# Fourier mixing and a squared-ReLU MLP on one core: a fourth x buffer, other load slots, the first x piece by SyncE's queue, and a new table

## The chip, the cores and the metric

The kernel runs on one core of a Trainium2 chip. The core has TensorE for matmuls (PE, with the weight load PEld shown apart), VectorE (DVE), ScalarE (ACT), GpSimd (POOL) and SyncE (SP), and 16 DMA engines that all DMA queues share. DMAs are issued here from two places: SP's queue (q1 in the profile, "hardware_dynamic") and POOL's queue (q0, "software_dynamic"). Only POOL's DMAs change the type on the way. The metric is device time of one execution in microseconds; lower is better.

## The reference

For each of 8 batches of 3008 rows by 256 columns: a real FFT along the rows, a complex 256 x 256 product with a bias, a soft threshold at 0.01 on the real and the imaginary part, and the inverse FFT. All 24064 rows then pass an MLP with 2048 hidden columns whose activation is `s * relu(h)**2 + b`.

```python
X = np.fft.rfft(x, axis=1)
Yr = Xr @ w_r - Xi @ w_i + b_r
Yi = Xr @ w_i + Xi @ w_r + b_i
Y = np.sign(Y) * np.maximum(np.abs(Y) - 0.01, 0)      # Yr and Yi alike
y = np.fft.irfft(Y, n=3008, axis=1)
r = np.maximum(y @ w_in, 0.0)
out = (s * (r * r) + b) @ w_out
```

## The kernel before

The FFT of 3008 points is split as 94 x 32. Each batch's x is held as 94 partitions (index n1) by 32 x 256 elements in fp16, in four chunks of 8 of the 32 positions. The first step is a matmul with A_t (94 x 96, the 94-point transform); the second goes through a detour in DRAM (u is written, read back as rows in `us`), is transformed with F_t, mixed with the weights, thresholded, transformed back with T_t, and goes through DRAM again (v written, `vs` read) to the last transform with C_t, which leaves yt, the MLP's input.

The program has two parts. `first_batch` does the whole transform of batch 0 while nothing else can run. It opens with 40 matmuls on a tile of ones (`keep_awake`), then eight groups of matmuls, one for each half chunk of x of batch 0, in that order, by edges that tie each group to the one before (`issue_after`), with five matmuls on ones behind each. ACT and DVE copy the result (ut) out. After the fourth group `place_w` copies w_st to W_t on ACT and the second part of F_c is loaded; after the sixth the big tables T_t, F_t and F_2 are loaded by SP, and F_t's landing gates POOL's loads of batch 1's x and of the MLP weights. Then comes the mix of batch 0 and what follows it.

`emit_load_x(0)` issues batch 0's x from POOL, eight pieces of 94 rows by 1024 columns, fp32 in DRAM and fp16 in the tile. Just ahead of it, A_t is issued on SP. Chunks 0 to 2 come from a pool of three buffers (`xpool`), chunk 3 from one of its own (`x2pool`). The pool `rpool`, tag "rt", has three buffers of 4 KB a partition: the two staging tiles w_st, then b_st, then the three `rt` tiles of the MLP's relus.

The second part is a loop over 47 tiles of the MLP (up to 512 rows each), 16 slots a tile, 752 slots in all, about 1.02 us each. Matmuls of the MLP are interleaved with those of the next batches' transforms: `plan` holds units of work by slot, `aside` holds loads by slot. `mark[b]` is the slot at which batch b's MLP tiles begin. In the loop that fills them, s0, s1 and s2 are the marks of batches b-2, b-1 and b; `s1_units(b)` are the first-step matmuls, `take_rows` the loads of `us` rows, `s23_units` the middle steps and `s4_units` the last. `load_x_later(b, c)` issues a chunk as two half-chunk DMAs from POOL.

What is not a matmul in this part (bank copies, relus, squares, the sums of a seven-product scheme for the second MLP matmul, stores, loads) is handed to `later` as a piece. The long string TURNS gives each piece, two characters in base 36, the engine that does it (ACT, DVE, SP or POOL) and how many pieces later it is emitted. From there each engine's order is as written (`manual_schedule`). The tag `psh` holds the first MLP matmul's two banks, `rt` the relu, `gt` its square; `s` and `gt` sums are DVE's or, as an accumulating DMA, POOL's (line 1317).

Of the kernel before, what the change touches and what calls it, by code (L numbers as in the profile page):

```python
# [11 lines left out]
F32 = mybir.dt.float32  # L12
# [14 lines left out]
    "1x1x261s291p1t221o291s1w291l1u2m2q2y321c1t1c1c25191c291d1s1c282w1o1t1k20353n6z3r6f173r111521"  # L27
    "101c0x111515141h1l14181k3o181l1x5m5m750x151h1l2e2q1u1i0g0t0g0s7x0p0t11192y1q2226080w2g0h110l"
    "111h1p3e2m2u220h0t0g1c0x1h212d2i2q3a3q0h101g0g250h3q4q0l191l1x2m3m321q0c0w1g0c0p0x1d292x3q32"
    "3y36101w091e0c0p1h0o390x1h1p252m323q3a0k0s1831523i0l0x111l1t212e2u3m36080m0c0w0k1829182o1519"  # L30
    "1h1t362u3m260o0s1p101s111h1l1x263a2i2q15321k2g154e3q0o151d25292t45453l0c0k1k0l0t1h21292h292l"
    "2t081e0d0i0g3h0h0s212h143i1g1m1k1n371g1s2g1h3e4m101a2i2q3m3q0w120s0x1s113q101p0x111g1l1m181h"
    "1g1k201l3i4y1h1m252t1c3x1h191c451c1c20191e1x11143p1x191k2814151c1q192q141o2g1d1l1k2h1h4u1c1p"
    "1p1o1x2d2p1g1x4236181824152e1865141l11161e1x2h143415182p1b1c301t151i181p291d141p1h1k291p1o24"
    "1l1n6j1k2d1l1l1k1o1h2p1x261h1t1c1w1f5v1h1p1x2d2m2u2y3i101g0x160w1h2h0x2l0w181d0x1n1o2o1t110s"
    "1t1z1x1l1x292d2u2i3e2y0g1w1110182d182p1d1g1w1d1f5b1p1o202p1l1x1g1x1h2y1g1o1h292t454i564i5a18"
    "1u0o180l0u0h1l29101g0l143h0r111g2s1d0p0s1f1p0w142l111h184a191l21252d2u2m3u2u0w200w3q0w1h100t"
    "101t1c201p2p113t141i1p26191g1w1d1t1w281x261f4b1d1h252l1h25393h4q423i4214240l0k6y0r0s3u0s2k0t"
    "0l0o0z0l0t0w1l1011141o2k191h1p293p4l294l292t1x2p0g0u0k200l0w1i0l102d0x1t0x19264i1e102y1g2h0w"
    "1g1y1k28192q1i15292t181k2k1h151e3e3m1f2k2u142s1h0x1l1d141p18191g1t2m2a1o1y1o2g1d1p1s291p1p24"  # L40
    "1p2y1o1t1s1y1o211p1q252h1k1o2w1t1k1z1k1s3g1t1l1o1z1x1h1s291p1p1q1o1x241k1t242o1p3e1l1p1o1p2h"
    "1p2t1c1l2y1h1g2h1d1i1g1w1h1m252l1o2g1l2t391j1g311t1d1620291n1d141o1h1w1w1x20241p3f7b1l1t1l1x"
    "1o1s1d1p2h461h1p1c1s1b5v191l1t213q262e2u0w1g0t0y0w1h2h0x2t0w181d0x1n1s1w1p0x0w1t1n1p1p1t2l2p"
    "3a3m2m3q0w1g150w191g14291t181s191b5j1x1h1k1w1x211h1p252a1k1o1h252l495m4i4q4y0x1q0w180t0y111l"
    "2d101g0x0w190z15142g1h0x141j1h101l3c142h1k46191h1p252l3u2u3u2u0o0w111a0w28190x181918202d3l11"
    "191d3a253a191g1k1d1l1o201l1q174b19251x2d1d2t3d3l3u4m3y460o1g0x0o4i0z0k3u182w0p0h0k0v110p0o18"
    "0w1519181w191h292h3h2x4d4d4l49292h0l3a0o1w0d0o120l0o210p3x0k111a1y1e0t6m0s2c0w102a1c1x1d3a2a"
    "1a1m0x1x2p181c2s1l1c1m363u1j282m0s2k190p2t150w1l190x14282m4i191i1428111l1l211t2l1c1t2q1g2l1h"
    "1q1c1s191i2h2t1d1k3d1p1g1v1g202s1x1h181z1p1g1o2k1l1x1q1s1t211o1w202s1x1m1t1x1o1w2p1l1x1l1t2y"
    "1t1k281l1q1o211l1q252l1o381l2c351j1g2x1x191a1c1x1r1h18251l1s1w1w24281p1r7b1x251h1p1o2o1p1x1l"  # L50
    "3u1g1t1g2k1f5v1d1h1l1t22262y2i0s1d0t2y0o1p2h0w2t0w281d0p1j0w2k1p0x101t1n1p1p2d2h3l3u424a4m08"
    "1s0t0x0w1h101p1p141k11137719181c1w191d1c1l1p3m1o2k1d1l1p293q463a260w160w1g0x260t1t2h182g0p0t"
    "290z1514251x11181z251k1s2o1g211s3m1d1p1t252d3e3m42260w18112e1g2s100t1c151g1t113d193p1c1q1x36"
    "191c1p1h1k1k241l1u1b4r181l212d1l2l353p4e4u4i3q0s380t0s160z0k160s1c150t0s171d11101t101d1k1o24"
    "1l1p1x2t41413d3d2t4h393h0w160w1c0l0t0y0p142l11450l11524m3q1m1y0u005y042410101e101p151u1i120t"
    "1t2h1014281h181i3a3e2p2d2m0o2h190l3l150w140x11141k2m3u1t1y1c28191d1g211d3d1w1h2q1g1l1k1q1g1t"
    "1h22292t1c1g3c1x1g231g1k341x1d1k231p1g1k2k1l1p1q1p1t2h1o1t1s2s1p1q1s1x1o1s251p2h1l253y1k1k28"
    "1h2a1k1x1h1i212h1k3c1h242l1f1c2w1x15161g211r1p18241p1t2g1s1t2c1x1n7f1g1x1x1h1s2o1p1p1x4e1g1t"
    "1c2k1f5z1d1h1l1t2u1y2e3e0s1d0t1i0o1p2h0w2x0w341d0p1j0w1o1t0x101d1r1p1p1x2d2d2q362m3e0c1w0t10"
    "102g181d211g211d1f5b211o1o3h1p291k1t1h1q1c1s1l1p2t454i5e4q4y151a0s1g0t160s1p29101g0p103t0r11"  # L60
    "1g2o1d0p0s1f1h0w1g2c0w19192a1d1h252l2x4m3m322q111c103e18240x111415141s1t2h0x3h151q1t2e15141s"
    "1g1p202g1p1y1f4j1h1p252p1l292x3t4i4q423m142c0l0k0y0r0w3y0w240x0p0s0z190x0w280x191c1c2o1d1l1p"
    "25412x2d4d2p3t3t250o2u0o210l0x3u0l0o350p210k1d2q0s0y0o2p0w141m182c1d221g292p1c1o2w1l1o1y3a3a"
    "452d2m1429190p2h150w1s0x1114281u3y1t221828191h1o1x1l21201p2y1c241l1u1g1x1d1u2h2t1k1s3o1p1d1v"
    "1g1o2k1x1h1k1z1x1l1c2l1p1t1m1t1w241l1s212k1p421o1t1k1o2g2h351d1h1q1c1d211c261g1s1d1i212d1o34"
    "1p202l351c301p155y181t1j19101p1h1k211p1o241x1n771g251l1l1k1s1h1p214q1h1t1c1s1b5v1d1h21253q32"
    "2i260s140p0u0l212h0w1l0s180p0t2t1c2g1p0x1c1l1n1p1h252l393u3e3y46081g0x0w191g141t19182d19135b"
    "1d141c1w191t1c1x212y1g291h1p2h3x4q564a3q0s1u0s180p0u0s1h1x101k0x142x0v0x1g2k1h110s311d141828"
    "191l1l6e1l1p1x2h2t3a4e3m2q0w19103i101k180t0s11181s1d2h0x3x141e1h2y0x181o151l1s201h1q174b1925"
    "252h192x3d3p3y4u4e3y0o340d0w4a0n0o0y0o180t0l0o0z1d0t0s1p10191g1k1w1h1x2d2p49354h414h412p2d0d"  # L70
    "120o180l0s2a0p101o0x410h1p565a1u080u0h2c0o0s1q181x19222a362u121a0p1p2d0w102w1d141e363e252c2m"
    "0k28110h2x110o281w11151h2q2y1x261g28151l1c251h2d1l1x2y1k1o212a1k1x1h26252t181g301t1k1z1k1k2w"
    "1x1h1k2x1p1g1p2k1k1l1m1p1o2g1l1t1s2s1p3u1l1p1p1o2g1l1p1g253a1h1h211c2e1g1s1d1i21291o2g192l2p"
    "1j1k2o1l1d5m20291f151c201h1p251o1o201l1o2p1x1l1k1s1l3h1l3e1h1p1c1o1h1l1t2132363e2a0w1k0t0y0w"
    "1p21182p1c2k1t15231c3g211h181t391p1t1x252h323q322e0s0w1110151g10291t1g25151l201k1x2l311o1x1p"
    "3a1c1o1h2h454h525i5a4e111q0o180p0y0k1h1p141k0p141d0v19183119111f1h0w141c1o1x1519252935424a3i"
    "320o1o103y101g11151d1c1k0x1h112h1p2y19102c181c1x191y1c25252h1l2t393h4q4a3i3q0s2k111b0o4m0o10"
    "110p140z111d0w201d141c2c191h1p2h353d3l392h293l290g1o0l0p0u0l0o2c0t2h1d461i1u220o28151x261g1t"
    "1d2i221q212l20142g1518223a3e2d1c2h1l0t1n1d1g1w1h1g1p363a1k1s1l1p1s211h1l1l1u1k1t1w211t222h2t"
    "1k1o3c1p1h1v1g1o3d251h1k231h1g1k291l1p1p1o2g1o1s212o1l1k211p1o2o1p2l1k1p1u1l1p291k4d411k1w1h"  # L80
    "1m1x291k24191j1g2h1p191x1l1c1w1d1g251o281p1x1o1x21251x261g241o211p1y252h1o2c1l1r1o2o1x1h391t"
    "1k1o1p1p1t1s1w1p1t1w2d1l1t1x221k211s1w1x2225291s2t1d1r1s2g1t1l1v1l1o211t1w241s2g1p1t1s281p1p"
    "212a1l1x1o1w1x2225251s2c1d2h1o2g1p1h1v1l1s241t1t1x1w201t1x20291p1t1t2e2y1u1u321c1l1o1s1l1q21"
    "291o2g191n1s2o1t1l2t1p1o1o1p1p1t1s2c1p1t1s251p1t212u1o1t1s1w1p1u25291o2t1d1r1s2s1t1l1v1l1o1s"
    "1t1t241s2h1p1t1t1s1t1y1w281s251p1q1x1y21261p1u1x1y"
# [64 lines left out]
def kernel(  # L150
# [51 lines left out]
    xpool = ctx.enter_context(tc.tile_pool(name="xp", bufs=3))  # L202
# [154 lines left out]
    def emit_load_x(b, chunks=range(N2 // XCH)):  # L357
        xv = x[b].rearrange("(n1 n2) d -> n1 (n2 d)", n2=N2)
        for c in chunks:
            if b < 2 and c == N2 // XCH - 1:  # L360
                t = x2pool.tile([P, XCH * D], F16, name="x2", tag="x2")
            else:
                t = xpool.tile([P, XCH * D], F16, name="x16", tag="x16")
            parts = 2 if b == 0 else 1
            w = XCH * D // parts
            for i in range(parts):
                nc.gpsimd.dma_start(
                    out=t[0:N1, i * w : (i + 1) * w],
                    in_=xv[:, c * XCH * D + i * w : c * XCH * D + (i + 1) * w],
                )  # L370
            x16[(b, c)] = t
# [12 lines left out]
    A_t = cpool.tile([P, 96], F16, name="A_t")  # L384
    nc.sync.dma_start(out=A_t[0:N1, :], in_=A_d)
    emit_load_x(0)
# [375 lines left out]
    def s1_units(b, more_banks=False):  # L762
# [6 lines left out]
        def unit(i):  # L769
# [6 lines left out]
            assert b < 2 or (b, c) in held[-3:]  # L776
# [729 lines left out]
    for c, at in enumerate((18, 18, 18, 55)):  # L1506
        aside.setdefault(at, []).append(
            lambda c=c: load_x_later(2, c, [] if c else [row_loads[(1, 3)]])
        )
# [4 lines left out]
    for b in range(2, B):  # L1514
# [4 lines left out]
        for q, at in enumerate((-9, -6, -1, 4)):  # L1519
# [6 lines left out]
        if b + 1 < B:  # L1526
            free_at = 37 + 4 * (mark[b] - s1 - 50) // 16
# [59 lines left out]
```

## Time and profile before

| | us |
|---|---|
| median of 3 runs (814.24 to 814.68) | 814.51 |
| the profiled execution | 814.47 |
| its span, first to last instruction | 812.4 |

| engine | busy us | share of the span |
|---|---|---|
| PE (matmuls) | 801.9 | 99% |
| DVE | 760.4 | 94% |
| ACT | 748.9 | 92% |
| POOL | 108.7 | 13% |

The profile is of one execution. A matmul's busy time overlaps with its neighbours', since matmuls are pipelined, so PE's 99% is a share of time in which some matmul is under way. A line such as "L225 PE MATMUL psf<-x,A_t" names the code line, the engine, and the tiles written and read; nearly all matmuls carry line 225, the helper's, and are told apart by their tiles. A wait "PEld L225 <- DVE gt L1325: 3.9, 9, 0.6" reads: weight loads waited for DVE's operation of line 1325 on gt, 3.9 us in total, 9 times, 0.6 us the longest. In a timeline an operation has its start, its length, its engine and, in brackets, how long its engine stood before it and for what. A line of a stretch gives its length, each engine's busy time with its number of instructions (PE, PEld, DVE, ACT, POOL), the granted clock of TensorE as a share, the busy share of the 16 DMA engines (over 1 where packets overlap) and GB/s.

### The profile page before, as it was taken

Reading aid. Unit: us, or ns where it says so; the run is one execution under the profiler, and the core shown is the slowest. Engines: PE = TensorE matmul, PEld = TensorE weight load, DVE = VectorE, ACT = ScalarE, POOL = GpSimd, SP = SyncE. Lnnn points to the kernel's source line nnn. Section 1 sums busy time; section 2 is a strip of 40 time slices with the busy share of each in tenths; the row PEclk is TensorE's granted clock in tenths of the full one; section 3 lists DMA queues with packets and bytes.
Section 4 is the critical chain, followed back from the end, with each engine's and each line's share of the span. In section 5 each row is a group of like instructions: output and inputs, shape, how many; then the busy total and the mean of one; then the engine's idle time right before and its main releaser. Section 6 shows DMA issues by size and latency. Waiting matters only on the chain.

```text
span 812.4 us, 22159 instructions
## 1 busy us (share of the span) xinstructions
PE 801.9 (99%) x9006; PEld 614.0 (76%) x9006; DVE 760.4 (94%) x1334; ACT 748.9 (92%) x938; POOL 108.7 (13%) x153
## 2 busy tenths in 40 slices
PE   8999999999999999999999999999999999999998
PEld 7857767777777967788677886778867788777876
DVE  5899999999999999999998999999999999999895
ACT  5989989999999999999999999999999999898884
POOL 4540000111111110121001210001100100010100
PEclk9999999999999999999999999999999999999999
DMA  8964385566856669467575875657654544632323
GB/s 201 182 173 89 92 243 150 115 138 166 222 122 120 151 154 232 100 123 179 121 209 113 158 153 145 169 125 143 140 162 117 141 98 115 176 70 54 78 55 90
DMA packets 121054, 113.42 MB, mean 140 GB/s; under 512 B 9965, under 2 KB 98161, under 8 KB 120953
## 3 DMA queue, kind: packets, MB, share of 16 engines
q1 hardware_dynamic: 102409, 80.55, 35.9%
q0 software_dynamic: 18544, 31.47, 24.0%
q8 instruction: 70, 1.15, 0.6%
q14 instruction: 31, 0.25, 0.1%
HBM read 53.52 MB, written 46.66 MB: 123 GB/s over the span
## 4 chain that ended last, share of the span: by engine, by line
PE 55%; DVE 3%; DMA 1%; issue 0%; DVEq 0%
PE psh L225 24%; PE psa L225 20%; PE psf L225 11%; DMA gt<-gt 1%; DVE gt L1325 1%; DVE ost L1390 1%; DVE ring L924 1%; DVE gt L1165 0%; DMA out_dram<-ost 0%; DVE v L288 0%; DVE u L288 0%; DVE s L1325 0%; DVE rt L1156 0%; DVE ost L1278 0%; DVE ring L907 0%
## 5 line engine op out<-in xcount | busy, mean ns | idle before, releaser
L225 PE MATMUL psh<-yt,w_in 128*128 128x512 f16 (+3 forms) x1792 | 444.5, 343 | 0.2 <-ACT rt L1154 0.2
L225 PEld LDWEIGHTS <-gt 128*128 128x128 f16 x4400 | 306.5, 98 | 143.8 <-DVE gt L1325 3.9
L1154 ACT ACTIVATE rt<-psh 128x1024 f32<-128x1024 f32 x347 | 355.0, 1025 | 25.6 <-PE psh L225 22.9
L1163 ACT ACTIVATE gt<-rt 128x1024 f16<-128x1024 f32 x259 | 272.2, 1061 | 3.4 <-DVE rt L1156 1.4
L225 PE MATMUL psa<-w_out_t,gt 128*128 128x128 f16 (+1 forms) x2208 | 199.9, 224 | 0.3 <-DVE gt L1165 0.3
L225 PEld LDWEIGHTS <-w_in 128*128 128x128 f16 x1824 | 151.9, 98 | 15.9 <-issue 1.5
L225 PE MATMUL psa<-T_s,gt 128*128 128x128 f16 x1824 | 144.2, 219 | 0.3
L1165 DVE TENSOR_TENSOR gt<-rt 128x1024 f16<-128x1024 f32 x117 | 141.2, 1217 | 2.5 <-ACT rt L1154 2.1
L1317 POOL DMA_DIRECT2D gt<-gt x65 | 56.5, 868 | 574.2 <-DVE s L1325 157.7
L1390 DVE SCALAR_TENSOR_TENSOR ost<-psa,s_bc,bias_bc 128x256 f32<-128x256 f32 x152 | 72.8, 479 | 7.8 <-PE psa L225 6.7
L1325 DVE TENSOR_TENSOR gt<-gt 128x1024 f16<-128x1024 f16 x107 | 73.0, 683 | 0.6
L1390 DVE SCALAR_TENSOR_TENSOR ost<-psa,s_bc,ost 128x256 f32<-128x256 f32 x129 | 61.7, 478 | 4.8 <-PE psa L225 4.0
L880 DVE TENSOR_TENSOR ring<-psf,s 128x512 f16<-128x512 f32 x84 | 57.6, 686 | 4.0 <-PE psf L225 2.5
L1325 DVE TENSOR_TENSOR gt<-gt,s 128x1024 f16<-128x1024 f16 x86 | 59.0, 686 | 1.2 <-PE psf L225 0.4
L1325 DVE TENSOR_TENSOR s<-gt 128x1024 f16<-128x1024 f16 x86 | 58.8, 683 | 0.4 <-ACT gt L1163 0.2
L225 PEld LDWEIGHTS <-s 128*128 128x128 f16 x688 | 45.4, 98 | 17.6
L225 PE MATMUL psa<-T_s,s 128*128 128x128 f16 x688 | 52.4, 219 | 0.0
L225 PE MATMUL psf<-W_g,xf 128*128 128x256 f16 x336 | 50.4, 273 | 0.0
L225 PEld LDWEIGHTS <-xf 128*128 128x128 f16 x504 | 44.8, 98 | 3.3
L350 POOL DMA_DIRECT2D x<-in_x_dram x48 | 32.3, 766 | 78.6 <-PE psa L225 39.6
L225 PE MATMUL psf<-x,A_t 94*96 94x512 f16 x103 | 39.3, 381 | 0.3 <-DVE u L288 0.2
L225 PE MATMUL psf<-C_t,vs 96*128 96x96 f16 x484 | 38.3, 205 | 0.9 <-DMA vs<-vd 0.6
(116 smaller groups left out, 839.4 us busy)
## 6 DMA issues: line engine op xcount, KB each, us to landing
out_dram<-ost SPq DMA_DIRECT2D x74, 256.0 KB
gt<-gt POOLq DMA_DIRECT2D x65, 256.0 KB, 4.0
ud<-u SPq DMA_DIRECT2D x56, 192.0 KB
us<-ud SPq DMA_DIRECT2D x28, 384.0 KB
vd<-v SPq DMA_DIRECT2D x42, 256.0 KB
vs<-vd SPq DMA_DIRECT2D x28, 384.0 KB
x<-in_x_dram POOLq DMA_DIRECT2D x56, 188.0 KB, 5.6
ring<-ring SPq DMA_DIRECT2D x120, 64.0 KB
```

What stands on the lines that cost most here:

```text
L225: return nc.tensor.matmul(out, lhs, rhs, **how)
L350: nc.gpsimd.dma_start(out=t[0:N1, i * w : (i + 1) * w], in_=xv[:, at : at + w])
L880: lambda e: nc.vector.tensor_tensor(out=ring[0][:, i % 4], in0=ps, in1=hold[i // 2][:, i % 2].unsqueeze(1).to_broadcast([P, 2, D]), op=ALU ...
L924: lambda e, o=o[:, k], a=a[:, k]: nc.vector.tensor_copy(out=o, in_=a),
L1154: nc.scalar.activation(out=rt, in_=ps, func=AF.Relu)
L1163: nc.scalar.activation(out=gt, in_=rr, func=AF.Square)
L1165: nc.vector.tensor_tensor(out=gt, in0=rr, in1=rr, op=ALU.mult)
L1317: nc.gpsimd.dma_start(out=a12, in_=a11, accum_op=ALU.add)
L1325: nc.vector.tensor_tensor(out=out, in0=a, in1=b, op=op)
L1390: ins = nc.vector.scalar_tensor_tensor(out=out(), in0=hold[of], scalar=s_bc[0:size], in1=other(), op0=ALU.mult, op1=ALU.add,)
```

## The change

There are four parts.

- `xpool` has four buffers in place of three, and the check that a chunk is still held looks back four chunks.
- The very first piece (batch 0, chunk 0, first half: 94 rows by 1024 columns) is loaded as fp32 by SP's queue into a staging tile x_st from `rpool`, and then converted to fp16 on chip: ACT copies the left half of its columns, DVE the right half. `emit_load_x(0)` now stands ahead of A_t's load, so x_st is the first DMA on SP's queue and A_t the second. POOL issues the other seven pieces as before.
- The loads are put at other slots: the last chunk of batch 2's x at slot 24 in place of 55; the third and fourth `us` row loads at -4 and -1 from the batch's start s1 in place of -1 and +4; the next batch's x chunks at -8, -6, 10 and 26 in place of 10, 14, 26 and some 48.
- TURNS is another table of the same length, 2693 pieces.

```diff
-    "1x1x261s291p1t221o291s1w291l1u2m2q2y321c1t1c1c25191c291d1s1c282w1o1t1k20353n6z3r6f173r111521"
...
+    "1t1t221o251l1p1y1k251o1s251h1q2i2q362q181p18181t151820181p1c203o1l201g1l294f7b1b3b1b3j15151h"
...
-    xpool = ctx.enter_context(tc.tile_pool(name="xp", bufs=3))
+    xpool = ctx.enter_context(tc.tile_pool(name="xp", bufs=4))
...
             for i in range(parts):
+                if (b, c, i) == (0, 0, 0):
+
+                    x_st = rpool.tile([P, w], F32, name="x_st", tag="rt")
+                    nc.sync.dma_start(out=x_st[0:N1], in_=xv[:, 0:w])
+                    for copy, q in ((nc.scalar.copy, 0), (nc.vector.tensor_copy, 1)):
+                        r = slice(q * w // 2, (q + 1) * w // 2)
+                        copy(out=t[0:N1, r], in_=x_st[0:N1, r])
+                    continue
                 nc.gpsimd.dma_start(
...
     A_t = cpool.tile([P, 96], F16, name="A_t")
+    emit_load_x(0)
     nc.sync.dma_start(out=A_t[0:N1, :], in_=A_d)
-    emit_load_x(0)
...
-            assert b < 2 or (b, c) in held[-3:]
+            assert b < 2 or (b, c) in held[-4:]
...
-    for c, at in enumerate((18, 18, 18, 55)):
+    for c, at in enumerate((18, 18, 18, 24)):
...
-        for q, at in enumerate((-9, -6, -1, 4)):
+        for q, at in enumerate((-9, -6, -4, -1)):
...
-            free_at = 37 + 4 * (mark[b] - s1 - 50) // 16
-            for c, at in enumerate((10, 14, 26, free_at)):
+            for c, at in enumerate((-8, -6, 10, 26)):
```

More of the change, by code (lines that the diff above doesn't have):

```diff
@@ L26 @@
 TURNS = (
-    "1x1x261s291p1t221o291s1w291l1u2m2q2y321c1t1c1c25191c291d1s1c282w1o1t1k20353n6z3r6f173r111521"
[L28 to L85, printed above, removed]
+    "1t1t221o251l1p1y1k251o1s251h1q2i2q362q181p18181t151820181p1c203o1l201g1l294f7b1b3b1b3j15151h"
+    "101p1x0w11150w201h0w14182w192h3h5m564v7j590l0p0x111m12221i000h042c7h0d0l0p0t1u121a1y040o1o08"
@@ new lines @@
+    "0p0d0t19213e262e2q050p0w2c0l1519212a2y3a2e080s280c0l2t3y4a090p0t1h2a2y2i1m081029090l0t1h2529"
+    "3m4e2q2e0w1g002i040o191c3811191h1x3i2u1y420o0w181p4y260h0t0x1d1h1x262u361y04360s180p0x2p141s"
+    "11151d1h3e2q2a2u0g111l0w1g111h1t292e3e2e2q0t360s182p363e0l0x19191h413p2x31080w1t0c0p151t2d2d"
+    "352t35081e080q0c350k0w1k2k101y111a1c1k1l2k2d2i32141e2i2u3i4i0w160t0s1p153i101o0x1x141g1i151g"
+    "1l1k1s1h3m4y191i1t2p111s1t10181v15203s141m1x0x102l1p191p2t14181c1m1d2q101c341f63191l1c1s1h3e"
@@ new lines @@
+    "175n1d1d1h181l212l3u0x1h1q2y0s0s1w0p260s450s1d0t0y161l210w2w0x1w2h0z0w2k1h0t0w1h3t1d0w1w1d1l"
+    "1s1l1p201t1j5z1c1l1l1l1k1o1h1x1l321g1p1g2c1h1h1p212i36222i0s1s0p0u0s2d2l1g310p340x1517141s1x"
+    "19101h1v1t1x252935423m4a320g1p0x0w101c101p15141k150z5r1l15181w1d21181l192y1k2k1h1h1p2d3e2i3q"
+    "2q0s3q0o110p0y0k1l2d0w1k0t0w3t0z151s2d1p0x0w1v1l1c1s201g1x1l3q191l1t1x2h3m3a4m2e0s180w161828"
+    "0x11141518201529151p196q1t1y19181s1c1h1s241h1q1h21212h19212l3d463y4m3a10240d0c4a0n0o0y0o2d11"
@@ new lines @@
+    "0l0o13150p0s1k0w0x101k2k191h1p2149354d3125312d250c2y0g100h0p0y0p102g1t3d0h1p4i2a1u0c0u0g2k0w"
+    "1d2i1g25151e1m11212h0w1g2c1d1g1q3a3u3l2d2m0s2g190l1d11101l101114282e3y191i1420111h1l1x1l2p1g"
+    "1p1y1c1g1h1u1k24191u2d2h1d1o3k1d1h1j1k1o2k1t1h1g1r1h1p1g2k1h1l1m1p1x2h1j5v1c1l1k201h3y1f5z1c"
+    "1p1d1c1o1t251615192q1d141w151a181l15161t29182w191c291b182w1l1114211j1h101t1d1o291p1o241l1n6z"
+    "1k1t1l1t1k1t1l2h1t1y1c1l181o1h1x25293m2q2y260w1g0t0y0w1x29102h14240p0x39102g1p0x101h1n1p1h1p"
@@ new lines @@
+    "29313q363q3y0c1k0x0w1019181x15141g150z6z1l19181o1p1x151l213a1g1k1d1l1x1x2a363e3m0w3q0w180l1y"
+    "0s1l2d14380h0l150r11142s1l0x141r1h141h2s1c251d421h1h1p2d2h3y3i2u2e0o0x0w3m101s0x0l0w1h0w1k21"
+    "2d0l3t0x2m1l260t0w1k141h1s241d1q1h1l2h2x1h1x293h463m464e10240h0g460r0s120s30190x0o17190t0w1l"
+    "101114182k191h1p212x4d2h2x3p1t1t2d0g6e0k1s0h0s2i0h0s2g1l3p0l111u164e0o420s290p191i141w111a1i"
+    "1m1u0p1p290k142o1d141i3a3a3h2d2i0k2c150d1d110k1t1d0x0w202q3u1x26142011191c25191l1w1h2y1c1s1g"
@@ new lines @@
+    "1q1p24151q2d2p181d381l1c1r1c1w2x1t19181v1l1c1l2g1g1p1i1o1o2h2j6f1d1h1g2o1d1e1f631g1l1c1g2k1d"
+    "1p2215191i1h14211d1i1k1s191i1t1x1g3015292917182x19111o21130t0w1p191o2c1o21281h1j771c2d1h1l1o"
+    "2k1d1h1t1y181l182c1h1l252d2m3m2m2u0w1k0t0y0p1p2h0t2l0w281d0p1n0w2k1t0x0w1p1r1p1p1x2l35424a3i"
+    "320c1l0t1010180x311h101c110v5b191g0w1h112d181p1x22101g19293p414e4m5e4u0w1m0w180l0u0l191l142w"
+    "0l0k0x0r0x0w30190p0w1f1p0s0w290x1d1g6q151d1t2d3h4u3y423e0w150w4u0w1c0s0t0w11141c0t1x0t290p2u"
@@ new lines @@
+    "113u0h0g100k11181k151q111x1x2l0x212x3d4i423e3q0g20050s460f0s3q0s2w0x0l0k0z150t0s1h0w0x10141s"
+    "191h1x254l2x3l292p3d3p2p0h1q0o100l0o0y0p142c39410l0x221m4m0y1y4m081y08250h112i101w0x1a1i1m0s"
+    "1t2d0s1c281d1c1m3q3u3125560s20150d1b11141h1l1118202a3y101a101w111d1h1o1h1t1h1p2q181l1c1m1c1o"
+    "1h222d2p1d1g351l1d1r1c1k2w1t1d1g1z1l1c1g2s1k1p1i1p1o1w1n6b1h1l1x2k1h3i1f4z1c1h181c2819292m11"
+    "151e140x201016181p191m1p251c301d2d2x1f101c1d0t1s2131150w1s191p281k1k241h1j771d1p1t1l1o2g1l1t"
@@ new lines @@
+    "1h321c1l1c2g1d1h1p2d2u323i2a0s190p0u0s1p2h0w2h0w1w1d0p1j0w381t0x1g1p1r1t1l1x2d353q3y4a320c0s"
+    "0t10111d143d1h101c110v571910182g1519181l192q14281d1h4d4l4u5i525i0t120o110l1210191t142s0l0k0x"
+    "0r0t0s2o150t0s170x0o0w2h0x1h142i0t191d252p3q463q4q0o1k0w4q0s1g150t111h141c2d2l0t290x1215260l"
+    "0o140t1g1k1w1h221h1x252l1925313h3q4a3y4e142c0l0k1m0r0s120s34110p0w171h11101p1419181g201h1p1x"
+    "252x3l3t2x311x3h1t0p4q0o100l0o3q0p0w2c1t3h0l0p320k0y0k250w191i181w0x1a11212p101k2w1l1k1y3a3u"
@@ new lines @@
+    "1j2c2m102g190l1d150w211g1115282e2i1c1m1824151h1l291p2p1k1l2u1g1k1l1u1k20191m292d1d1o301d1h4t"
+    "1g1k291p1d1c1r1h181o2d1l1p1i1k1l1s2b5z181l1c1s1h46175f1d1p19181t1h212q101h1q0w101s101i141h11"
+    "1i1p25182s1d1s2t1f102p1d0t1l1x2d150s1w191g1w1p24281p1j6z1h2l1h1t1k2g191p1d42181l182l1d1h1l1t"
+    "263a2i220s180t160o252l102h102w150t1f0w2s1p15141l1n1t1h1p292h3a3q2i36081o11111024111d1p102s15"
+    "17571d1w1c1x191d1g1p1x261k2l191l1x4l4q52565a0o1m0s1g0p0u0s1h1t141w0p0o3t0v0t0s1o190t0x1f110s"
@@ new lines @@
+    "181s0x2118720t111x2d2p2u4a3a2q0h1c0s4q0s1w0p0t0w0x0w1k2d310p2l0x1i0x1i0x0w1c0x1d1c1w1d1i1g1t"
+    "212l191h3d3p3y424a4i1020110g0q170s3y0w1c150p0p171d0t18200s151d1024191h1p214l294125292x2l2l0c"
+    "220w1w0h0s1a0h0s28313p0p1h4y1i4y0t5y0o2g0p111a0w1p1122321e1i1y0q0c1h250c102k19101e323e35292i"
+    "0g250x09190t0c1s100t10281y2i1t221824151h1l211p2p1k1t2i1g1k1l1u1k21191y292h1c1k381h1g1n1k1o3d"
+    "1t1h1g1v1l1c1l211g1l1m1o1o2c1l1o1s2g1h3a1h1p1h1k2g2h2t2215191e1c1128142a1g1x1d1i212d1k301h20"
@@ new lines @@
+    "2l1f1c2o1p151c251n1d141x1h1s201o1p241p1o211l1p1s251p391l1u1g1t1k1s1l1p1x2d3m2u322a101k0x1210"
+    "1h29142l18241d111n14381t1h1o1x1x1h1t292h313i323y3m0k0w0x0x0w1c111l151424111t141c2t111p1d1x1p"
+    "1u1c1s1l252d455m4q5246105y0w1g0t0y0w1d1h101s0p142d0r110s20110p13150p0s290w1p15151h2d314e3y36"
+    "3e0g0w191i0s100p141h181o0x25141h1136191c1o1h1p1w1p1y1c1l212h1h212t354a3u363e0o100t13143m101k"
+    "110t0w13151d141g191h1k1w1h1l1t213x2x253d3l251t1t0s1s0p0s2y0p0o1w152t193y1a3e1e0k240l191m1820"
@@ new lines @@
+    "151i1m1q212h1k0x2s151s1y3236290w281h0t1j190w1s1d1h2036361c1t1d1h1k241h1p1d1m181l1s241p1u2d2h"
+    "1d1o381d1h1j1k1o2d1p1h1k1v1h1g1o2c1p1p1p1o1x1l1s1s291p1p1p1o1s1w1x2d1h1p2q1p1g211h39411c1o19"
+    "1e1t211g20151f1c2g1l19291l1c1g1h1h211o2d1l1t1k1s1l1x1x2u1g1t1k1o1p1u1x251k28151n1o2d1t1h2p1l"
+    "1k1w1h1k1p1o2l1l1p1o1w1l1l1p1u1s1s1t1w1p1y21251o28191n1o291t1h2p1l1k1x1l1k1o1o2c1l1p1o241l1l"
+    "41421h1l1k1o1h1m1t1x1g2d151f1g1o1h192p1d1g1w1d1c1p1o1w1l1t1w291l1p1p2u2e1u1m1u141h1k1s1l1y21"
@@ L86 @@
+    "211o2k19391k1s1l1d2d1h1h1t1h1g1k1o281l1p1o1x1l1x3l3q1g1l1k1o1h1m1t1x1g24151f1g2d1h192d1d1g1w"
+    "1h1k2c1o1s1l1p1p1t1x1y1k241o211l1m1t1u1x221l1q1t1u"
 )
```

## The prediction

> **What bounds the kernel now.** I read the page first (busy shares, the 40 slices), then the waits, the timeline of the first 15 us, stretches of the DMA engines, and the chain of waits last.
>
> ```profile
> span 812.4 us, 22159 instructions
> ...
> PE 801.9 (99%) x9006; PEld 614.0 (76%) x9006; DVE 760.4 (94%) x1334; ACT 748.9 (92%) x938; POOL 108.7 (13%) x153
> ```
>
> TensorE (PE) is the bound. What a change can win or lose is time in which PE stands. By stretch, from the windows:
>
> ```profile
> 1.90:2.25 0.35, 0.35 (x6) 0.35 (x5) 0.35 (x1) 0.10 (x1) 0.35 (x2) 1.00 0.15 31
> ...
> 5.40:8.50 3.10, 1.59 (x26) 1.24 (x26) 0.91 (x2) 0.96 (x2) 1.28 (x4) 1.00 1.09 205
> 8.50:12.00 3.50, 3.49 (x40) 3.44 (x41) 1.60 (x5) 2.26 (x5) 0.79 (x1) 0.51 1.11 203
> 60.00:812.40 752.40, 746.48 (x8399) 569.69 (x8397) 711.43 (x1243) 702.47 (x859) 81.58 (x112) 1.00 0.58 136
> ```
>
> The last three numbers are granted clock, DMA share and GB/s. PE stands half of 5.4 to 8.5, then runs 3.4 us at half clock, while the DMA engines are full (over 1.00). After 60 us it hardly stands: adding up, over all matmuls, how far the next start lies beyond the usual distance for that shape gives 7.5 us lost after 60 us and 10.5 us before. The waits after 60 us name the sums on VectorE first:
>
> ```profile
> PEld L225 <- DVE gt L1325: 3.9, 9, 0.6
> ...
> PEld L225 <- issue: 2.0, 9, 0.3
> ...
> PEld L225 <- DMA vs<-vd: 0.8, 1, 0.8
> ```
>
> No wait for an x tile is among them. In the head it is otherwise; the timeline has:
>
> ```profile
> 0.73 0.30 SPq L385 DMA_DIRECT2D A_t<-dft_first  x1
> ...
> 1.09 0.56 SPq L391 DMA_DIRECT2D w_st<-in_w_r_dram  x1
> ...
> 1.25 4.25 POOL L367 DMA_DIRECT2D x<-in_x_dram  x8 [0.82 <-POOLq L1571]
> ...
> 5.40 0.34 PE L225 MATMUL psm<-A_t,x 94*128 94x96 f16 x4
> ...
> 7.59 0.34 PE L225 MATMUL psm<-A_t,x 94*128 94x96 f16 x4 [1.40 <-DMA x<-in_x_dram]
> ...
> 13.58 0.34 PE L225 MATMUL psm<-A_t,x 94*128 94x96 f16 x4
> ...
> 14.50 1.92 PE L225 MATMUL psm<-W_t,ut 128*128 128x256 f16 x16
> ```
>
> Eight groups of x matmuls run in a fixed order, each when its piece has landed; the mix of batch 0 starts at 14.5. Everything later hangs on it. One more view, the DMA engines from 1.5 to 2.27 us, where A_t alone is in flight:
>
> ```profile
> DMA packets 67, 0.01 MB, mean 17 GB/s; under 512 B 67, under 2 KB 67, under 8 KB 67
> ...
> q1 hardware_dynamic: 67, 0.01, 8.1%
> ```
>
> 8.1% of 16 engines over 0.77 us is 15 ns a packet, but the share from 1.90 to 2.25 is 0.15: two or so of 16 engines work. The packet records say the same: A_t's 94 rows come in two trains of 47, a packet every 11.7 ns, 1.82 to 2.48. C_t's 96 rows, of the same 192 bytes on the same queue, come in trains of six (96/16).
>
> **The change part by part.** *The first piece on SyncE's queue.* It removes one POOL issue (0.52 us) and a piece of 94 rows from POOL's stream, and puts 94 rows of 4,096 bytes at the head of SP's queue, ahead of A_t, both w_st, b_g and F_c. The disputed cost is how many engines carry it. The nearest row is A_t's: same partitions, same queue, two engines; I take that. Then each of two engines carries 47 rows, 192.5 KB, while it also carries POOL's other seven pieces, 6 rows each (94/16), 42 rows, 172 KB read.
>
> Rates: T_t's undisturbed 3,072-byte packets took 121 ns, 25.4 KB/us an engine. In the full stretch 7 to 12 us POOL's queue wrote 0.93 MB of fp16 (1.86 MB read) and SP's 0.10 MB: 1.96 MB over 80 engine-us, 24.5 KB/us. x_st is issued in A_t's place at 0.73, its first packet is due at 1.85 (A_t's: 1.82). Until POOL's first packet at 3.13 it moves 1.28 x 25.4 = 32 KB; 160 KB are left. From 3.2 to 5.2 us both queues had work:
>
> ```profile
> q0 software_dynamic: 116, 0.20, 61.4%
> q1 hardware_dynamic: 317, 0.31, 45.5%
> ```
>
> SP's queue (q1) got 0.31 of 0.71 MB read, 44%. At that share POOL's 172 KB are out after 12.6 us, x_st then lacks 24 KB (0.95 us): it lands at 3.13 + 12.6 + 0.95 = 16.7 us. The Trainium skill (DMA: Bandwidth & Descriptors, section Queues, rings and completion order) says that an engine takes turns between queues a packet at a time; with both sides' packets 4,096 bytes that is half each, 160/12.25 = 13.1 us, and the landing comes at 16.2 and the sum below 0.5 us lower. The trace's 44% is near that, with SP's packets smaller there. I go by the measured 16.7. The bounds: all of SP's first gives 1.85 + 192.5/25.4 = 9.4; all of POOL's first gives 3.13 + 7.0 + 6.3 = 16.4, so 16.7 is about the late end.
>
> *Behind it.* A_t, needed by the same first matmul, follows on the same two engines: 0.55 us. The conversion is one ACT and one DVE copy of 512 columns side by side; the ACT row is W_t<-w_st, 621 ns; DVE's copy isn't shown, between 0.28 (x f16 adds of 256 columns) and 0.69 us. Both end near 17.3, against 5.40 for the first x matmul now. The w_st loads follow, 32 packets an engine at 46 ns, 1.5 us, landed by 19; place_w needs them after the fourth group, about 21.5, so they cost nothing. b_g and F_c are small and needed after the sixth. If the two copies stood ahead of DVE's fills (0.48 + 0.17 + 0.70 + 0.27 us) in its order, up to 1.6 us more; those fills wait for nothing, so I take none.
>
> *The eight groups then.* All other pieces have landed, so groups run at PE's pace: 0.66 us at full clock (11.99 to 12.65), 1.16 at half (8.51 to 9.66). PE has stood from 5.4 on; after a far shorter stand it ran at half clock for 3.4 us, so three groups are slow: 3 x 1.16 + 4 x 0.66 to the last group's start, and 0.9 to the mix (13.58 to 14.50) = 7.0. The mix starts at 17.3 + 7.0 = 24.3, not 14.5: +9.8 us. A longer slow stretch (the one from 1.04 to 5.13 took 4.1) adds up to 1.5 us.
>
> *What follows the mix* shifts whole. w_in is issued at 20.46, lands in 15.3 and is needed at 44.6, some 9 us of cover, but its issue waits on F_t, loaded after the sixth group, so both move together. The 3.7 us that PE loses from 20 to 60 us go to copies of banks by ACT and DVE, which shift along, so nothing there gives time back.
>
> *Four x buffers, loads at other slots.* A slot is about 1.02 us. The chunks go from slots +10, +14, +26, some +48 to -8, -6, 10, 26 around each batch's start, the last rows from -1, +4 to -4, -1. No matmul waits for x after 60 us: gain 0. The issues stay 48 on POOL (0.77 us) and 28 on SP. They run ahead of the accumulating gt loads on POOL, which is 13% busy; five transitions will hold two x halves among the row loads. The longest gt<-gt landing now, 8.7 us, cost PE 0.3 us; if each of the five paid twice that, +3; I take 0, since most land in 4.0 us with none.
>
> *The table.* Decoded by operation: 8 relus and 15 bank copies go from ACT to DVE, 18 squares from DVE to ACT, one sum copy to DVE, two adds from POOL to DVE. ACT: -8 x 1.025 + 18 x 1.061 - 16 x 0.585 = +1.5 us; DVE: +8 x 1.220 - 18 x 1.217 + 16 x 0.684 + 2 x 0.686 = +0.2. Both stay under PE. What it does to the 7.5 us lost after 60 us can't be read from before: between -4 (half of it gone) and +5; I take 0.
>
> Sum: +9.8. The profiled execution took 814.47 us (span 812.4), the median of three is 814.51; the forecast is 824.3.
>
> **Rivals.** *SP's queue goes first.* x_st lands at 9.4, POOL's rows on its two engines end at 9.4 + 7.0 = 16.4, and the last group starts there instead of 13.58: +2.9, 817.4. For it: x_st is queued first. Against: the shared stretch above.
>
> *The piece spreads over 16 engines* (not slower). For it: w_st, 128 rows on the same queue, took the share from 0.15 to 0.46 as it began. Then x_st takes about a microsecond, uses the idle stretch from 1.85 to 3.13, and leaves POOL one piece less of 94 x 177 ns / 16 = 1.0 us: the last group starts some 0.9 sooner, 813.6. The decision lies at about eight engines: x_st's 94 rows would then be in before 5.4 with room. The Trainium skill (same page, section Issuing engine by pattern) calls SP's and ACT's queues generally faster and names SP for simple loads; that rule would give this case. Against it A_t's two trains stand.
>
> *The stalls after 60 us go* with the new table: at most -7.5, which would leave +2.3 of my sum; it lies inside the other cases' ranges.
>
> **How the numbers follow.** The two-engine landing with shared queues has 0.70 (819 to 829: landing and clock +/-2, table -4 to +3). SP first has 0.15 (815.5 to 820). The spread has 0.14, 0.08 of it with a table gain of over 0.7 that takes it past 0.2% (1.6 us, about what this measurement can tell from no change), 0.06 within. Anything beyond has 0.01. So faster 0.08, same 0.06, slower 0.86. A range of 816 to 829 leaves out the spread and the tails, under 0.2.
>
> **What would show it.** Right: the DMA share near 0.13 from 1.9 to 3.1 us, the first x matmul past 14 us with a wait for the conversion behind x<-in_x, half clock after it, eight groups without DMA waits, the mix near 24, and the same time from there to the end as now, 800 us within 4. Wrong: a share of 0.9 from 1.9 on and the first x matmul by 6 us; or a first matmul near 10 with waits between groups; or, with the head as said, PE waits after 60 us that differ from 7.5 by more than 5.

## The result and the profile after

The changed kernel takes 823.11 us (median of 5 runs, 822.07 to 823.33), against 814.51 us before; the ratio is 1.010, 95% interval 1.0085 to 1.0115. It is slower by 8.6 us. The profiled execution took 823.33 us, span 821.6; the one before 814.47, span 812.4.

The page of the changed kernel begins:

```profile
span 821.6 us, 22127 instructions
...
PE 799.8 (97%) x9006; PEld 614.6 (75%) x9006; DVE 759.8 (92%) x1343; ACT 750.4 (91%) x933; POOL 107.5 (13%) x150
```

The matmuls are the same 9006; the span has grown round them. Stretches of the changed kernel, in the columns of the stretches before (length, busy time by engine, granted clock, DMA share, GB/s):

```profile
1.90:3.10 1.20, 1.20 (x14) 1.20 (x13) 0.58 (x1) 0.10 (x1) 1.20 (x4) 1.00 0.22 39
3.10:12.00 8.90, 1.75 (x23) 1.57 (x20) 0.00 (x0) 0.00 (x0) 3.93 (x7) 0.74 0.96 187
19.10:24.50 5.40, 5.36 (x61) 5.36 (x61) 2.23 (x5) 2.76 (x6) 0.00 (x0) 0.50 0.07 19
24.50:26.90 2.40, 2.28 (x46) 2.10 (x44) 2.12 (x12) 2.31 (x6) 0.00 (x0) 1.00 0.22 61
62.00:821.60 759.60, 754.98 (x8485) 576.70 (x8483) 721.03 (x1265) 713.55 (x866) 79.59 (x108) 1.00 0.57 136
```

From 3.1 to 12 us PE works 1.75 of 8.9 us, and that is the last of the matmuls on ones. The timeline of the head says what it waits for:

```profile
0.73 0.36 SPq L370 DMA_DIRECT2D x_st<-in_x_dram  x1
1.15 0.28 SPq L394 DMA_DIRECT2D A_t<-dft_first  x1
...
1.94 10.16 SPq L399 DMA_DIRECT2D w_st<-in_w_i_dram  x1
...
15.24 0.62 ACT L373 CAST x<-x_st 94x512 f16<-94x512 f32 x1 [13.23 <-DMA x_st<-in_x_dram]
15.24 0.42 DVE L373 CAST x<-x_st 94x512 f16<-94x512 f32 x1 [12.76 <-DMA x_st<-in_x_dram]
...
19.14 0.48 PE L225 MATMUL psm<-A_t,x 94*128 94x96 f16 x4 [14.30 <-DMA A_t<-dft_first]
...
23.79 0.53 PE L225 MATMUL psm<-A_t,x 94*128 94x96 f16 x4
...
24.75 0.34 PE L225 MATMUL psm<-A_t,x 94*128 94x96 f16 x4
...
26.96 1.23 PE L225 MATMUL psm<-W_t,ut 128*128 128x256 f16 x7 [0.18 <-ACT ut L237]
```

The first piece lands 14.5 us after its issue, A_t, behind it, not before 19.1, and the mix of batch 0 starts at 26.96 instead of 14.50: 12.5 us later. That is more than the 9.2 us by which the span grew. Summing, as in the prediction, how far each matmul's next start lies beyond the usual distance for its shape gives 23.6 us lost in the head (10.5 before, up to 15.5 us past the first MLP matmul) and 3.8 us after it (7.6 before). So 13.1 us went into the head and 3.8 came back from the other parts of the change. The waits of PE after 62 us show the same; these lines answer to those of before:

```profile
PEld L225 <- DVE gt L1333: 2.4, 7, 0.5
...
PEld L225 <- issue: 1.0, 3, 0.5
...
PEld L225 <- DMA vs<-vd: 0.4, 1, 0.4
```

The wait for VectorE's sums on gt (line 1325 before, 1333 now) went from 3.9 to 2.4 us, the stands called "issue" from 2.0 to 1.0, the wait for vs from 0.8 to 0.4.

### The profile page after: what moved, and what is told of

Read it like the earlier page. It is cut to its first block, busy times and chain, and to the rows that moved or that the text cites. A ratio compares the mean times of both kernels' runs of the same rounds, so it can differ in the third digit from the quotient of the medians.

```text
span 821.6 us, 22127 instructions
## 1 busy us (share of the span) xinstructions
PE 799.8 (97%) x9006; PEld 614.6 (75%) x9006; DVE 759.8 (92%) x1343; ACT 750.4 (91%) x933; POOL 107.5 (13%) x150
## 4 chain that ended last, share of the span: by engine, by line
PE 88%; ACT 2%; DVE 1%; DMA 1%; issue 1%; SPq 0%; ACTq 0%; DVEq 0%
PE psh L225 38%; PE psa L225 32%; PE psf L225 18%; ACT rt L1162 1%; DMA vs<-vd 1%; DVE gt L1173 1%; ACT gt L1171 0%; DMA out_dram<-ost 0%; DVE u L288 0%; ACT u L288 0%; DVE ost L1286 0%; ACT v L288 0%; DVE vs L288 0%; SPq L792 0%; DVEq L1286 0%
## 5 line engine op out<-in xcount | busy, mean ns | idle before, releaser
L1162 ACT ACTIVATE rt<-psh 128x1024 f32<-128x1024 f32 x339 | 347.0, 1025 | 23.6 <-PE psh L225 21.3
L1171 ACT ACTIVATE gt<-rt 128x1024 f16<-128x1024 f32 x277 | 289.6, 1059 | 3.3 <-DVE rt L1164 1.0
L1173 DVE TENSOR_TENSOR gt<-rt 128x1024 f16<-128x1024 f32 x99 | 120.6, 1222 | 2.4 <-ACT rt L1162 2.1
L225 PEld LDWEIGHTS <-s 128*128 128x128 f16 x688 | 45.4, 98 | 17.6
L1164 DVE TENSOR_SCALAR rt<-psh 128x1024 f32<-128x1024 f32 x37 | 45.0, 1220 | 3.2 <-PE psh L225 1.6
```

The costliest lines, as they stand in the source:

```text
L225: return nc.tensor.matmul(out, lhs, rhs, **how)
L1162: nc.scalar.activation(out=rt, in_=ps, func=AF.Relu)
L1164: nc.vector.tensor_scalar(out=rt, in0=ps, scalar1=0.0, scalar2=None, op0=ALU.max)
L1171: nc.scalar.activation(out=gt, in_=rr, func=AF.Square)
L1173: nc.vector.tensor_tensor(out=gt, in0=rr, in1=rr, op=ALU.mult)
```

## The experiments

Each is compared with runs of the kernel before on the same chip; their median was 814.09 us for the first four, 814.44 for the next four and 814.14 for the last two.

**The two halves apart.** First the head alone, put into the kernel before:

```diff
+                if (b, c, i) == (0, 0, 0):
+                    x_st = rpool.tile([P, w], F32, name="x_st", tag="rt")
+                    nc.sync.dma_start(out=x_st[0:N1], in_=xv[:, 0:w])
...
+    emit_load_x(0)
     nc.sync.dma_start(out=A_t[0:N1, :], in_=A_d)
-    emit_load_x(0)
```

> The kernel before with one part of the change: the first x piece goes through SyncE's queue as fp32 and is converted on chip, ahead of A_t's load; three x buffers, old slots, old table. Theory (the change is two parts of opposite sign: the head costs the 12.4 us by which the mix of batch 0 starts later in the changed kernel, 26.9 against 14.5; the table and slots give some 3.5 us back after 60 us): 814.5 + 12.4 = 826.9 us, the first x matmul at 19.1, the mix at 26.9. Rival (the head costs only the 8.6 us seen at the end, because part of its delay is absorbed by later work whatever the table): 823.1 us.

Measured: 826.50 us (825.69 to 827.36), ratio 1.0152, interval 1.0126 to 1.0177: +12.4 us. First x matmul at 18.7, mix at 26.2. Nothing that comes later absorbs the head's delay.

Then the rest alone, the changed kernel with the first piece back on POOL's queue:

```diff
-                if (b, c, i) == (0, 0, 0):
...
-                    continue
...
-    emit_load_x(0)
     nc.sync.dma_start(out=A_t[0:N1, :], in_=A_d)
+    emit_load_x(0)
```

> The changed kernel with the first piece put back on POOL's queue behind A_t's load as before: four buffers, new slots and new table stay. Theory (rest gains what the matmul starts lose less after 60 us, some 3.5 us): 811.0 us, mix at 14.5. Rival (the rest brings nothing and the head's delay is partly absorbed): 814.5 us.

Measured: 810.27 us (810.18 to 810.64), ratio 0.9952, interval 0.9937 to 0.9968: -3.8 us, mix at 14.47. The sum of both, +8.6, is the whole change. This version beats both kernels.

**Why the first piece is late: the number of DMA engines.** One load of 94 rows becomes two:

```diff
-                    nc.sync.dma_start(out=x_st[0:N1], in_=xv[:, 0:w])
+                    for rows in (slice(0, 80), slice(80, N1)):
+                        nc.sync.dma_start(out=x_st[rows], in_=xv[rows, 0:w])
```

> The changed kernel with x_st's one load of 94 rows split in two loads on the same queue, rows 0 to 79 and rows 80 to 93. Theory (the cost is the number of DMA engines: 94 rows ride on two, 80 rows on 16 at five each and 14 rows on 14 at one each): x_st has landed by about 5 us, the first x matmul starts before 6.5, the mix at 13.5 to 15, time 809 to 812 us. Rival (staging as fp32 by SyncE's queue and converting on chip is slow in itself, however many engines carry it): no more than 2 us better than the changed kernel, 821 or above.

Measured: 813.84 us (812.94 to 814.54), ratio 0.9995, interval 0.9986 to 1.0004: 8.9 us better than the changed kernel by the differences from before, with the same bytes on the same queue. The timeline of its head:

```profile
0.72 0.89 SPq L371 DMA_DIRECT2D x_st<-in_x_dram  x2
...
4.49 1.28 ACT L374 ACT_TABLE_LOAD   x1 [4.49 <-DMA x_st<-in_x_dram]
4.51 0.42 DVE L374 CAST x<-x_st 94x512 f16<-94x512 f32 x1 [2.03 <-DMA b_g<-in_b_i_dram]
...
7.62 0.33 PE L225 MATMUL psm<-A_t,x 94*128 94x96 f16 x4 [2.38 <-DMA A_t<-dft_first]
...
11.59 0.50 PE L225 MATMUL psm<-A_t,x 94*128 94x96 f16 x4 [1.99 <-DMA x<-in_x_dram]
...
17.30 0.61 PE L225 MATMUL psm<-W_t,ut 128*128 128x256 f16 x4 [0.18 <-ACT ut L237]
```

x_st has landed by 4.5 instead of 15.2 us. From 1.9 to 3.1 us, before most of POOL's traffic, SP's queue had this share of the 16 DMA engines, first in the changed kernel and then with the split:

```profile
q1 hardware_dynamic: 34, 0.05, 21.9%
...
q1 hardware_dynamic: 88, 0.32, 85.5%
```

That is 3.5 engines' time against 13.7. Even of the 3.5 the larger part is w_st's, whose rows moved beside x_st: 30 of the 34 packets are w_st's, 4 are x_st's. The number of engines is the cause of most of the delay. But the mix starts at 17.3, not the expected 13.5 to 15, and the time is 1.8 us above the expected 809 to 812. Three reasons stand in the lines: ACT's table load, which began at 0.72 before, now waits behind x_st; A_t, still 94 rows, is last at 7.6; and the third group waits until 11.59 for a piece of POOL's. The last comes from an order that the change altered without saying so: with the first piece gone from POOL's queue, the tile scheduler issues chunk 3's two pieces and the two small bias loads ahead of chunks 1 and 2.

**A_t's place.** In the changed kernel, with x_st on its two engines, A_t's load ahead of it:

```diff
-    emit_load_x(0)
     nc.sync.dma_start(out=A_t[0:N1, :], in_=A_d)
+    emit_load_x(0)
```

> The changed kernel with A_t's load issued ahead of x_st's on SyncE's queue. Theory (behind x_st, A_t's 94 rows of 192 bytes share two engines with POOL's queue packet by packet and land 4 us after x_st; ahead of it they land by 2.5 us): x_st lands some 0.6 us later, the first x matmul at 16.4 instead of 19.1, time 820.3 us. Rival (the first x matmul waits for the conversion, and A_t's late landing costs nothing): 823.1 us.

Measured: 819.77 us (819.23 to 820.57), ratio 1.0070, interval 1.0049 to 1.0090, 2.9 us better than the changed kernel by the differences from before:

```profile
15.40 0.62 ACT L373 CAST x<-x_st 94x512 f16<-94x512 f32 x1 [13.40 <-DMA x_st<-in_x_dram]
...
16.07 0.50 PE L225 MATMUL psm<-A_t,x 94*128 94x96 f16 x4 [11.37 <-ACT x L373]
```

x_st lands within 0.2 us of the same time, and the first matmul now follows the conversion. A_t's place cost 3.1 us, as the theory has it.

**The half clock.** In the changed kernel, more matmuls on ones:

```diff
-        last_pe = keep_awake(40)
+        last_pe = keep_awake(280)
```

> The changed kernel with 280 matmuls on the tile of ones at the start in place of 40, so that TensorE works on until x_st is converted. Theory (4.6 of the eight groups run at half clock after the long stand and cost 0.5 us more each): 2.3 us less, 820.8 us, all eight groups 0.62 to 0.66 us apart. Rival (the groups are paced by copies, not by the clock): 823.1 us.

Measured: 820.69 us (820.30 to 821.15), ratio 1.0079, interval 1.0066 to 1.0092, 2.4 us better than the changed kernel by the differences from before. The groups stand 0.62 us apart from the first on (18.89, 19.52, 20.14), and the mix is at 24.77. From the first group to the mix it is 5.9 us instead of 7.8. The other 0.25 us come from the first group, which starts that much earlier:

```profile
18.89 0.34 PE L225 MATMUL psm<-A_t,x 94*128 94x96 f16 x4
19.52 0.34 PE L225 MATMUL psm<-A_t,x 94*128 94x96 f16 x4
...
24.77 0.39 PE L225 MATMUL psm<-W_t,ut 128*128 128x256 f16 x2 [0.73 <-ACT ut L237]
```

**Can SyncE's queue win at all?** All costs found in the head, but for the half clock, taken away at once:

```diff
+                    for rows in (slice(0, 80), slice(80, N1)):
+                        nc.sync.dma_start(out=x_st[rows], in_=xv[rows, 0:w])
...
+                with tc.issue_after(issued[-1].ins) if b == 0 and issued else nullcontext():
+                    issued.append(nc.gpsimd.dma_start(
...
+    warm = cpool.tile([1, 1], F16, name="warm")
+    nc.scalar.copy(out=warm, in_=ones[0:1, 0:1])
+    nc.sync.dma_start(out=A_t[0:N1, :], in_=A_d)
     emit_load_x(0)
-    nc.sync.dma_start(out=A_t[0:N1, :], in_=A_d)
...
+        with tc.issue_after(issued[-1].ins):
+            nc.gpsimd.dma_start(out=b_h[64 * i : 64 * i + 1], in_=bv.unsqueeze(0))
```

> The changed kernel with every cost found in the head taken away at once: A_t ahead of x_st, x_st in two loads of 80 and 14 rows, POOL's seven pieces kept in the order in which the groups use them with the two bias loads behind, and ScalarE's table load brought forward by a copy of one element. Theory (the DMA engines are full from 3 to 12 us whichever queue carries the piece, so SyncE's queue can win only what it moves before 3.1 us): first x matmul at 5.4 to 6.5, mix at 13.5 to 14.5, time 809.3 to 810.5 us, at most 1 us from the run with the piece on POOL's queue (810.3). Rival (the staged piece itself costs, by its conversion and the wait for it): 812 us or above.

Measured: 811.50 us (810.70 to 813.86), ratio 0.9972, interval 0.9963 to 0.9982: -2.9 us from before. The first x matmul is at 6.22, inside the range, but the mix is at 15.54 and the time is 1 us above it: just short of the rival's 812. Against the version with the piece on POOL's queue (0.9952 and, below, 0.9961) it loses 0.9 to 1.6 us, by medians of different chips. So the gain of 2.9 us is no more than the rest of the change brings alone, and none is shown for SyncE's queue. The groups from the third on wait for POOL's pieces:

```profile
6.22 0.34 PE L225 MATMUL psm<-A_t,x 94*128 94x96 f16 x4 [1.20 <-ACT x L375]
...
8.42 0.34 PE L225 MATMUL psm<-A_t,x 94*128 94x96 f16 x4 [0.78 <-DMA x<-in_x_dram]
...
9.66 0.34 PE L225 MATMUL psm<-A_t,x 94*128 94x96 f16 x4 [0.45 <-DMA x<-in_x_dram]
...
15.54 0.72 PE L225 MATMUL psm<-W_t,ut 128*128 128x256 f16 x5
```

From 3 to 12 us its two queues had this share of the 16 engines:

```profile
q0 software_dynamic: 697, 1.20, 74.4%
q1 hardware_dynamic: 846, 0.84, 33.1%
```

The kernel before had 89.0% and 20.8% in the same stretch, and 1.99 MB against 2.04. The engines are full either way; the w_st loads now come after x_st and share them with POOL's pieces, whose last lands at 14.4 instead of 13.5. That w_st is the reason is argued from the shares; it wasn't tried apart. Neither was the half clock, which ran from 11.2 to 14.6 us here and from 8.5 to 12.0 before.

**Where the 3.8 us come from.** The table holds an engine and a number for each piece of work; pieces are issued in the order of their own number plus the table's. So the old order and engines can be written down for the new slots, and the new ones for the old slots. New slots and four buffers with the old order, written as a new table (its lines are left out here):

```diff
...
-    xpool = ctx.enter_context(tc.tile_pool(name="xp", bufs=3))
+    xpool = ctx.enter_context(tc.tile_pool(name="xp", bufs=4))
...
-        for q, at in enumerate((-9, -6, -1, 4)):
+        for q, at in enumerate((-9, -6, -4, -1)):
...
-            for c, at in enumerate((10, 14, 26, free_at)):
+            for c, at in enumerate((-8, -6, 10, 26)):
```

> Four x buffers and the new load slots with the table of before: every operation keeps its engine and its place in the order of before, only the moved loads take the places of the new table; the head is as before. Theory (the new table alone brings the gain of 3.8 us; no matmul waited for x or rows after 60 us): 814.1 us within 0.8. Rival (earlier loads bring it): 810.3 us.

Measured: 815.07 us (813.78 to 817.53), ratio 1.0013, interval 1.0005 to 1.0022: no gain, if anything 0.6 to 1 us lost. The new table with the old slots, an edit of the table's lines alone:

```diff
 TURNS = (
-    "1x1x261s291p1t221o291s1w291l1u2m2q2y321c1t1c1c25191c291d1s1c282w1o1t1k20353n6z3r6f173r111521"
...
```

> The kernel before, with three x buffers, the old slots and the old head, and the new table's engines and order for every operation but the moved loads, which keep the places of before. Theory (the new table alone brings the gain): 810.3 us within 0.8. Rival (it needs the earlier loads): 814.1 us.

Measured: 811.41 us (810.74 to 811.69), ratio 0.9964, interval 0.9951 to 0.9977: -3.0 us. Whether the slots add anything on top was then run side by side, five rounds each:

> The same kernel as the changed one with the first piece on POOL's queue (four buffers, new slots, new table), once more, side by side with the table alone. Theory (the earlier loads add nothing of their own): the two agree within 0.5 us, some 3.3 us under the kernel before. Rival (the earlier loads add 0.8 us to the table's gain, as the medians of two chips have it): this one is 0.8 us or more faster than the table alone.

> The same kernel as the table alone (three buffers, old slots), beside the one with the new slots on the same chip. Theory: within 0.5 us of it. Rival: 0.8 us or more slower, with the stand of TensorE at the first batch's last step (1.7 us between 100 and 120 us) as the place.

Measured: 810.76 us (810.09 to 811.50), ratio 0.9961, interval 0.9948 to 0.9973, with slots and buffers; 810.94 us (809.97 to 812.45), ratio 0.9960, interval 0.9947 to 0.9974, without. They agree within 0.2 us, and each is known to about 1 us: the table makes the gain, the earlier loads none that shows in the time. Some 1.5 us of the gain lie in the wait for VectorE's sums, 3.9 us with the old table (also with the new slots) and 2.4 us with the new one. The stands called "issue", 2.0 us with the old table, are not in the four profiles of the new table with the old head. The second profile of the table alone had waits for vs<-vd that the version with new slots has only for 0.4 us:

```profile
PEld L225 <- DMA vs<-vd: 2.7, 2, 2.0
PE psf L225 <- DMA vs<-vd: 2.4, 2, 1.8
PEld L225 <- DVE gt L1325: 2.4, 7, 0.5
```

The medians show no such loss. This execution took 812.45 us, the slowest of its five; the first profile of the table alone, at its median of 811.41 us, waited 1.8 us in the first of these lines. Why the rest of it costs nothing is open.

## Why the prediction was right, and where its parts were not

**The direction and its cause** were right: 824.3 was forecast, 823.11 came. The step that carried it, that 94 rows on SyncE's queue ride on two engines as A_t's had done, is shown by the split load: the same bytes land by 4.5 instead of 15.2 us. Neither rival was right: SP's queue did not go first (x_st lands at 15.2, not 9.4), and the piece doesn't spread by itself. The third, that the new table takes the stalls after 60 us away, came half true, beside the forecast and not in its place.

**The landing of x_st** was put at 16.7 us, by the 44% that SP's queue had got before; it came at 15.2. From 6 to 12 us the queues moved:

```profile
q0 software_dynamic: 628, 0.98, 95.8%
q1 hardware_dynamic: 41, 0.16, 7.3%
```

SP's 0.16 MB in 6 us on two engines are 13.3 KB/us an engine, more than half of the 24.5 that the prediction worked with. By the half share of the rule that the Trainium skill states (DMA: Bandwidth & Descriptors, Queues, rings and completion order: turns packet by packet), the landing would have been 16.2; the trace agrees with turns better than with the 44%, and is still 1 us earlier; why is open. The bound beside it, 16.4, was worked out with 25.4 KB/us and the 16.7 with 24.5, which is how the term came to lie past its own late end.

**A_t behind it** was the worst-sized term: 0.55 us was put, 3.9 measured (15.2 to 19.1). The prediction had POOL's rows out by 15.7, so A_t would run alone. They weren't: because x_st had more than its 44%, POOL's rows on those engines were late. The packet records have 41 rows of POOL's begun after 14.5 us, the last at 18.3. From 15.3 to 19.0 us:

```profile
q1 hardware_dynamic: 233, 0.09, 9.8%
q0 software_dynamic: 38, 0.07, 9.4%
```

POOL's 9.4% of 16 engines over 3.7 us are 5.6 engine-us, 2.8 of 3.7 us on each of two, while A_t's small rows took turns with them: in the packet records, 45 of A_t's 94 rows begin from 14.5 to 18.1 us, about one for each of POOL's, and the other 49 in the 0.6 us behind. The first x matmul came at 19.1, not 17.3. A_t moved ahead took 3.1 us off, which shows that its place made the delay.

**The eight groups** took 7.8 us to the mix, not 7.0: the half clock lasted 5.3 us after the first of them (to 24.5), over four groups and a half, not three. With TensorE kept busy the kernel took 2.4 us less, some 1.9 of them in these groups.

**Costs set to nothing.** The conversion took 0.62 and 0.42 us, inside the bounds, and all fills but one of 0.27 us ran ahead of it. SP's queue itself stood 10.2 us in the issue of the second w_st, which the prediction didn't see; with A_t first that stand is absent and x_st lands no sooner, so it cost nothing of its own here. The altered order on POOL's queue wasn't seen either; it cost nothing while x_st came last, and showed only once x_st was early.

**The slots and buffers** were put at 0, and are 0 within 1 us. **The table** was put at 0 between -4 and +5 and is worth -3.0 to -3.2 alone, -3.4 to -3.8 with the slots, near its end. So two terms missed in opposite ways: the head cost 12.4 us where 9.8 stood, the table and slots gave 3.8 where 0 stood. That the total came within 1.2 us is luck; its parts were off by 2.6 and 3.8.

**The signs.** Half clock and eight groups without DMA waits came as named; from the mix to the end it took 794.6 us against 797.9 before, which is within the 4 us. Three signs did not come: the mix was at 26.96 and not near 24, the first x matmul waited last for A_t and not for the conversion, and the DMA share from 1.9 to 3.1 us was 0.22 and not near 0.13, since rows of w_st were moving by then beside x_st.

## What to carry to other kernels

Before a load is moved to another queue, look in the trace at a load of the same number of rows on that queue, and at how many engines carried it: here that number made most of the delay, and a split of 94 rows into 80 and 14 was worth 9 us. What stands behind a slow load on its engines, however small, can pay too: 17.6 KB paid 3.9 us here. And a change of several parts is timed part by part: here one part was worth keeping (810.3 to 810.8 us) and the other hid it.

## What the runs showed of the hardware that was not expected

- A load of 94 rows of 4,096 bytes on SyncE's queue took 14.5 us from issue to landing beside POOL's traffic; as 80 and 14 rows it took 3.8 us (4.4 behind A_t's load).
- Behind that load and A_t's, the issue of the second w_st load on the same queue took 10.16 us instead of 0.47 (9.7 in two other runs), and the queue's next DMAs waited with it. With A_t's load ahead of x_st's it took 0.47 us. The reason isn't shown.
- 17.6 KB of small rows took 3.9 us behind it, sharing two engines with larger packets of the other queue; alone, before, their packets took 0.7 us from first to last.
- How long TensorE stays at half clock after a long stand varies: 5.3 us in the changed kernel's profile, 3.6 with the head alone (18.7 to 22.3), 4.7 with A_t first (16.1 to 20.8).
